# An early expert's units and its rest's run, reordered into one pipeline of turn, next up product, down product

## The chip, the cores and the metric

The kernel runs on 1 core of one Trainium2 chip. Its time is device microseconds (us) of one execution: 428.04 us is the median of three runs (427.71 to 428.32). Fewer is better.

## The reference

Three layers follow each other. The inputs are float32.

```python
# 1. attention in a sliding window: q, k, v (2, 8, 576, 64)
scores = q @ k.T / sqrt(64), kept where 0 <= i - j < 64; softmax; @ v
x = heads laid side by side -> (1152, 512)
# 2. mixture of experts: w_gate (512, 8), w1 (8, 512, 1024), w2 (8, 1024, 512)
logits = x @ w_gate; e = argmax(logits); gate = softmax(logits)[e]
row i goes to expert e[i], at most cap = 288 rows per expert, in order of i
out[i] = gate[i] * (relu(x[i] @ w1[e]) @ w2[e]), or 0 for a row past cap
# 3. dense layer: w_in (512, 2048), w_out (2048, 512)
h = x @ w_in; g = h * clip(h + 3, 0, 6) / 6; out = g @ w_out
```

## The kernel before, in words

**Attention and routing.** The rows go through the attention in nine blocks of 128. The operations are nodes of a planner written in the kernel (`node`, `run_nodes`): each has a priority, an estimated cost on TensorE (PE), ScalarE (A), VectorE (V), GpSimd (P) or the DMA queue (D), the nodes that it needs, and a ring of buffers that it takes and frees. The planner picks the node that can start first by its own clock and writes it into the engines' queues. Each engine then runs its queue in that order.

**The early expert.** After five of nine blocks (`NE = 5`) the expert with most rows so far is known. Its first 128 rows are gathered, scaled, turned (transposed by TensorE, `early_turn`) into `xTE`, and its weights, 8 half weights of 512 KB, are loaded into `wE` (tile `early`). An expert has four units (`NFU = 4`) of 256 hidden columns. A unit is an up product (`early_up`, two nodes `e0`, `e1`, of two chunks each), a relu to the tile `first_w` (`early_relu`, `er`), two transposes of the hidden rows (`early_hidden`, `et`), a copy (`early_hidden_out`, `eh`) and a down product (`early_down`, nodes `e2`, `e3`). These products are in full float32. The first `NEU = 2` units are nodes of the planner. The other two are written by hand after it: `own_up` (up product and relu) and `own_end` (transposes, copy, down product).

**The rest's run.** When all nine blocks are routed, experts are ranked (`ranks`, `slots`, `slot_index`), and the rows that the early expert's rank still has (`REST`) are gathered (`first_gather`, node `g0`, tile `first_w`). `rest_turn` scales them on VectorE and turns them into `xTR`. The run then uses the same eight half weights again: four units of `own_up` and `own_end` with `rest = True`. The order by hand is: up product of one unit, then `own_end` of the unit before it; `rest_turn` stands between the up product of the last early unit and the `own_end` of the one before. In three of the rest's units `own_end` also scales and turns a block of rows of the first team (`between`: `prep_scale`, `prep`). Behind each of the rest's units come three steps of `aside`, the index arithmetic of the compact order, on VectorE.

**The teams and the dense layer.** The other seven experts run in three teams (`TEAMS`), each a large expert ("w", `ws_stage`, two steps per unit) beside one or two small ones ("a", "b", `ts_stage` or `tiny_stage`), in the order of the strings `ORDER`. Their matrices are split: a float32 half weight in a buffer `raw` (8 of them, `NRAW`) is cast to a reduced format on ScalarE (line 252) and the remainder taken on VectorE (line 257), into `wt`, and a product is three passes. Last comes the dense layer (`d_stage`); its weights are first made out of 64-bit words by six operations on ScalarE and VectorE (`conv64`, lines 200 to 223), then split. Units 0 and 1 of the dense layer are loaded and made early, between the experts' units, at the places `FIRST_AT` and `SECOND_AT`; they are tiles `wt_fixed` and `first_w`.

**What orders the loads and splits.** From here on a second planner keeps an estimate of each engine's time (`est`, `spend`). Loads, conversions and splits are jobs with a due unit. `fill(limit)`, called wherever an engine will wait anyway, writes jobs into the queues as long as they start by the estimate before that limit; it does this only while `live[0]` is set. `need` forces a job out when a product wants it. A load counts as landed 3.5 us after its issue (`load_job`, `conv_job`).

Of the kernel before, what the change touches and what calls it, by code (L numbers as in the profile page):

```python
# [23 lines left out]
def tile_kernel(ctx, tc, q, k, v, w_gate, w1, w2, w_in, w_out, out, cap):  # L24
# [74 lines left out]
    def bank(tag):  # L99
        n = BANKS[tag][turn_at[tag] % len(BANKS[tag])]  # L100
        turn_at[tag] += 1
        return banks[:, n, :]
# [129 lines left out]
    NFU = F // FU  # L232
# [35 lines left out]
            nc.sync.dma_start(t.rearrange("p (k d) -> p k d", d=DM), src)  # L268


    NEU = 2
    x2f = xp2.tile([128, 2 * NC * XW], F32, name="early", tag="x2")
    wE = [x2f[:, HALF * i : HALF * i + HALF] for i in range(2 * NFU)]
    xTE, xTR = (
# [40 lines left out]
    with ExitStack() as actx:  # L315
# [25 lines left out]
        for i in range(2):  # L341
            r = slice(64 * i, 64 * i + 64)
# [53 lines left out]
        def node(name, prio, engs, fn, needs=(), take=None, free=(), lag=LAG):  # L396
            engs = {e: c * CS.get(name[0] if isinstance(name, tuple) else name, 1.0) for e, c in engs.items()}
            nodes[name] = (prio, engs, fn, needs, take, free, lag)
# [59 lines left out]
        box = {}  # L458
# [359 lines left out]
        def early_up(u, i):  # L818
            def run(e):
                if i == 0:  # L820
                    box["uE", u] = bank("s")[:, 0:FU]
                pairs = [(xTE[:, c, :], wE[2 * u][:, c * FU : c * FU + FU]) for c in (2 * i, 2 * i + 1)]
                mm(box["uE", u], pairs, start=(i == 0), stop=(i == 1))

            return run

        def early_part(u):
            return slice(FU * (u % 2), FU * (u % 2) + FU)
# [13 lines left out]
        def early_hidden(u):  # L842
            def run(e):
                box["vE", u] = pt = bank("s")[:, 0:FU]
                hf = box["hfE"][:, early_part(u)]
                for kf in range(2):
                    nc.tensor.transpose(pt[:, 128 * kf : 128 * kf + 128], hf[:, 128 * kf : 128 * kf + 128], ident)

            return run
# [42 lines left out]
                node(("wl", u, h), p + 2 * u + h, {"D": 1.3}, early_load(u, h), ["pl"], lag=2.0)  # L892
        for u in range(NEU):
            o = p + PRIO["ear"] + 2 * u
            node(("e0", u), o, {"PE": 0.86}, early_up(u, 0), ["xE", ("wl", u, 0)], "s")
            node(("e1", u), o, {"PE": 0.86}, early_up(u, 1), [("e0", u)])
            node(("er", u), o, {"A": 0.27, "V": 0.34}, early_relu(u), [("e1", u)], None, [("s", ("e0", u))])
            node(("et", u), o, {"PE": 0.22}, early_hidden(u), [("er", u)], "s")
            node(("eh", u), o, {"A": 0.27, "V": 0.34}, early_hidden_out(u), [("et", u)], None, [("s", ("et", u))])
            needs = [("eh", u), ("wl", u, 1)] + [("e3", u - 1)] * (u > 0)  # L900
            node(("e2", u), o + 1, {"PE": 0.86}, early_down(u, 0), needs, None if u else "x")
            node(("e3", u), o + 1, {"PE": 0.86}, early_down(u, 1), [("e2", u)])

# [108 lines left out]

    NWT = 4
    NRAW = 8
    FIRST_AT = (0, 4, 4, 4)
    SECOND_AT = (7, 7, 17, 19)
    NPC = 4
    EOFF = (mybir.EngineType.Activation, mybir.EngineType.DVE)
# [21 lines left out]
        steps.append((kind, s, f, unit_of[key], last))  # L1040


    ORDER = ('wwawwawawaww', 'awawwwwawaww', 'awbwwbwaaawbbwww')
    for n, (small, b) in enumerate(TEAMS):
        at_ = dict.fromkeys("abw", 0)
        order = ORDER[n]
# [24 lines left out]
    def spend(e, cost, ready=0.0):  # L1071
        est[e] = max(est[e], ready) + cost
        return est[e]
# [43 lines left out]
    def take_raw(m, h):  # L1117
        r_raw.take()
        raw_t[m, h] = rawp.tile([128, HALF], F32, name="raw")

    def load_job(m, h):
        _, s, u = units[m]

        def gate():
            return r_raw.free(raw_at[m, h])

        def run(e, fin):
            take_raw(m, h)
            if u == 0:
                e_of[s] = expert(s)  # L1130
            weights_in(raw_t[m, h], e_of[s], u, h)
            raw_ready[m, 2 * h] = raw_ready[m, 2 * h + 1] = fin + 3.5
            if whole(m):
                half_ready[m, h] = fin + 3.5
            return fin

        return [({"D": 1.46}, gate, run)]

    def conv_job(m, i):
        u = units[m][2]  # L1140
        ix = {}
        first = m == dense0 + 1
        b, (load, c_abs, c_round, *mid, t_add) = conv64(u, i, first_w[i] if first else None)

        def run_load(e, fin):
            r_raw.take()
            load()
            raw_t[m, i] = first_w[i] if first else b["lo"].bitcast(F32)
            return fin + 3.5

        def run_abs(e, fin):
            ix["ct"] = r_ct.take()
            c_abs()
            return fin

        def plain(fn):
            def run(e, fin):
                fn()
                return fin + 0.13

            return run

        def run_add(e, fin):
            t_add()
            r_ct.rel[ix["ct"]] = fin
            if first:
                r_raw.rel[raw_at[m, i]] = fin
            raw_ready[m, i] = fin + 0.2
            return fin + 0.2

        now = lambda: 0.0
        ops = [({"D": 1.46}, lambda: r_raw.free(raw_at[m, i]), run_load), ({"A": 0.6}, r_ct.free, run_abs)]
        ops.append(({"A": 0.57}, now, plain(c_round)))
        ops += [({"V": c}, now, plain(fn)) for c, fn in zip((0.34, 0.34, 0.61), mid)]
        ops.append(({"V": 0.61}, now, run_add))
        return ops
# [54 lines left out]
    def advance(fits):  # L1231

        for j in jobs:
            costs, gate, run = j[2][0]
            r = gate()
            if r is None:
                continue
            r = max(r, j[3])
            e = min(costs, key=lambda e: max(est[e], r) + costs[e] + BIAS.get(e, 0.0))
            t = max(est[e], r)  # L1240
            if not fits(j, e, t, costs[e]):
                continue
            j[3] = run(e, spend(e, costs[e], r))
            j[2].pop(0)
            if not j[2]:
                jobs.remove(j)
            return True
        return False
# [67 lines left out]
    def prep_scale(s, i, ready=0.0):  # L1316
        x_ready[s, i] = scale(xg[s, i], 3 * RANKS[s] + i, ready)
# [544 lines left out]
        ring.rel = [t] * ring.n  # L1862
    for _ in range(NFIRST):
        assert advance(lambda j, e, t, c: e == "D")

    spend("D", 0.8, done["g0"] - 2.3)
    for n, (s, i, _) in enumerate(rows_at[:3]):
# [17 lines left out]
    def own_up(rest, u):  # L1885

        key = "uR" if rest else "uE"
        t = xTR if rest else xTE
        box[key, u] = bank("rot")[:, 0:FU]
        mm(box[key, u], [(t[:, c, :], wE[2 * u][:, c * FU : c * FU + FU]) for c in range(NC)])  # L1890
        r = spend("PE", 1.83, box["rR"] if rest else done["wl", u, 0]) + 0.2
        fill(r)
        nc.scalar.activation(box["hfE"][:, early_part(u)], box[key, u], AF.Relu)
        return spend("A", 0.27, r) + 0.2

    def own_end(rest, u, r):
        pt = bank("rot")[:, 0:FU]
        hf, h = (box[n][:, early_part(u)] for n in ("hfE", "hE"))
        for kf in range(2):
            nc.tensor.transpose(pt[:, 128 * kf : 128 * kf + 128], hf[:, 128 * kf : 128 * kf + 128], ident)  # L1900
        r = spend("PE", 0.22, r) + 0.2
        fill(r)
        nc.scalar.copy(h, pt)
        r = spend("A", 0.27, r) + 0.2
        for fn in between.pop((rest, u), []):
            fn()
        if rest and u == 0:
            box["aR"] = bank("acc")
        acc = box["aR" if rest else "aE"]
        pairs = [(h[:, 128 * kf : 128 * kf + 128], wE[2 * u + 1][:, DM * kf : DM * kf + DM]) for kf in range(2)]  # L1910
        mm(acc, pairs, start=(rest and u == 0), stop=(u == NFU - 1))
        r = spend("PE", 1.75, max(r, done["wl", u, 1])) + 0.2
        fill(r)
        if u == NFU - 1:
            key = "yR" if rest else "yE"
            box[key] = y = first_w[2 if rest else 3]
            nc.scalar.copy(y, acc)
            box[key, "at"] = spend("A", 0.52, r) + 0.2

    between = {}  # L1920
    for n, (s, i, _) in enumerate(rows_at[:3]):
        between[True, n] = [
            lambda s=s, i=i, n=n: prep_scale(s, i, done["g0"] + 2.2 * (n + 1)), lambda s=s, i=i: prep(s, i, "t")
        ]
    before = None
    for rest, u in [(False, u) for u in range(NEU, NFU)] + [(True, u) for u in range(NFU)]:
        r = own_up(rest, u)
        if not rest and u == NFU - 1:
            rest_turn()
        if before:  # L1930
            own_end(*before)
        if rest:
            for _ in range(3):
                next(aside)
        before = rest, u, r
    own_end(*before)
    for step_, key, off_at in ((0, "yE", None), (1, "yR", lambda: off_of(REST))):
        at(step_, to_dense, box[key], off_at, box[key, "at"])
    x2 = xp2.tile([128, 2, NC, XW], F32R, name="x2", tag="x2")
# [67 lines left out]
```

## Time and profile before

| | before |
|---|---|
| median of three runs | 428.04 us |
| profiled execution | 429.9 us |
| its span, first to last instruction | 428.2 us |
| TensorE busy | 406.6 us, 95% |
| VectorE busy | 281.3 us, 66% |
| ScalarE busy | 234.1 us, 55% |
| GpSimd busy | 49.7 us, 12% |
| mean granted TensorE clock | 0.992 |

Rows below are from this one execution. PE is TensorE's matmul, PEld its weight load, DVE VectorE, ACT ScalarE, POOL GpSimd, SPq the queue of SyncE, which issues the loads. A row of a timeline has the start, the time to the end of the last instruction in it, the engine, the line of the kernel, the operation, what it writes and reads, and how many instructions were merged; in square brackets the idle time of the engine before it and who ended that. Matmuls are pipelined, so a row's time is a little longer than the distance to the next row; that distance is what a product takes. Line 238 is the helper of all matrix products, so the tiles tell them apart.

### The profile page before, as it was taken

To read this page: it belongs to the slowest core of one execution; us is meant where nothing else is said; L and a number is where in the kernel's file an instruction comes from. 1 tells how busy PE (TensorE), PEld (TensorE's weight loads), DVE (VectorE), ACT (ScalarE), POOL (GpSimd) and SP (SyncE) were. 2 spreads that over 40 slices of the span, in tenths; PEclk is the share of its full clock that TensorE was granted. 3 is DMA by queue.
4 is the path that set the end of the run, shared out by engine and by line. 5 is a ranking of instruction groups with operands and counts; after the bars stand their busy time and mean duration, and the time that the engine had idled before them with its cause. 6 is when DMAs were issued, how large, how long until landed. Compare 5 with 4: busy or idle time off the path is not lost.

```text
span 428.2 us, 8357 instructions
## 1 busy us (share of the span) xinstructions
PE 406.6 (95%) x3031; PEld 343.7 (80%) x3031; DVE 281.3 (66%) x781; ACT 234.1 (55%) x510; POOL 49.7 (12%) x108
## 2 busy tenths in 40 slices
PE   7999788898999999999999999999999999999992
PEld 4877565455899899899889898888888888898981
DVE  2888967479779857977579999548896222322440
ACT  4877773466576737657687666348583222423330
POOL 8633404011001101000000000000000000120101
PEclk9999999899999999999999999999999999999998
DMA  9998766973568996989940090023410000110101
GB/s 172 210 219 193 265 231 212 372 218 114 197 200 273 282 337 201 341 267 325 312 150 2 21 364 10 0 94 104 149 51 0 2 0 0 51 49 2 49 27 55
DMA packets 63857, 65.49 MB, mean 153 GB/s; under 512 B 30688, under 2 KB 47072, under 8 KB 63808
## 3 DMA queue, kind: packets, MB, share of 16 engines
q1 hardware_dynamic: 62224, 59.79, 45.6%
q0 software_dynamic: 1584, 5.08, 3.3%
q8 instruction: 26, 0.43, 0.4%
q14 instruction: 23, 0.19, 0.1%
HBM read 60.15 MB, written 4.72 MB: 151 GB/s over the span
## 4 chain that ended last, share of the span: by engine, by line
PE 84%; DVE 8%; ACT 4%; issue 1%; DMA 1%; SPq 0%; POOL 0%; ACTq 0%; POOLq 0%; DVEq 0%
PE banks L238 71%; PE banks L1459 2%; PE banks L498 2%; PE banks L1484 2%; PE banks L616 2%; ACT pe L588 1%; PE banks L562 1%; DMA v_sb<-in_v_dram 1%; PE banks L598 1%; DVE neg L575 1%; PE banks L1295 1%; PE banks L528 1%; ACT wt L252 0%; DVE raw L223 0%; DVE c L216 0%
## 5 line engine op out<-in xcount | busy, mean ns | idle before, releaser
L238 PE MATMUL banks<-x,wt 128*128 128x320 f32 (+3 forms) x432 | 79.8, 336 | 0.0
L238 PEld LDWEIGHTS banks<-x,wt 128*128 128x128 f32 x432 | 70.8, 188 | 7.1
L257 DVE TENSOR_TENSOR wt<-raw,wt 128x512 fp32r<-128x512 f32 x100 | 64.6, 686 | 17.6 <-ACT wt L252 15.3
L238 PE MATMUL banks<-wt,g 128*128 128x512 f32 x288 | 69.6, 390 | 0.0
L1548 DVE SCALAR_TENSOR_TENSOR gf<-r,banks 128x320 f32<-128x320 f32 (+3 forms) x48 | 26.6, 554 | 60.6 <-ACT r L1545 60.5
L1545 ACT ACTIVATE r<-banks,c_three 128x320 f32<-128x320 f32 (+3 forms) x48 | 28.0, 583 | 69.7 <-PE banks L238 69.6
L238 PEld LDWEIGHTS banks<-wt,g 128*128 128x128 f32 x288 | 53.7, 188 | 10.6
L252 ACT CAST wt<-raw 128x512 fp32r<-128x512 f32 x100 | 58.8, 629 | 5.4 <-PE banks L238 3.2
L238 PE MATMUL banks<-xT,wt 128*128 128x256 f32 (+2 forms) x288 | 38.4, 283 | 0.0
L238 PE MATMUL banks<-h,wt 128*128 128x256 f32 (+2 forms) x288 | 37.1, 279 | 0.0
L238 PEld LDWEIGHTS banks<-xT,wt 128*128 128x128 f32 x288 | 35.0, 192 | 1.9 <-DVE h L1355 0.8
L238 PEld LDWEIGHTS banks<-h,wt 128*128 128x128 f32 x288 | 34.6, 192 | 0.3 <-issue 0.3
L1554 DVE TENSOR_TENSOR g<-gf,g 128x320 fp32r<-128x320 f32 (+2 forms) x40 | 23.4, 584 | 10.4 <-ACT g L1551 9.6
L1551 ACT CAST g<-gf 128x320 fp32r<-128x320 f32 (+2 forms) x40 | 21.3, 533 | 14.6 <-DVE gf L1548 14.5
L1591 POOL DMA_INDIRECT out_dram<-raw,cidx x4 | 4.2, 1040 | 206.4 <-DVE raw L1585 197.9
L238 PE MATMUL banks<-x,wt_fixed 128*128 128x320 f32 (+3 forms) x144 | 26.8, 337 | 0.1
L200 ACT ACTIVATE c<-raw 128x512 f32<-128x512 f32 x32 | 21.6, 675 | 7.4 <-DVE raw L223 5.9
L238 PEld LDWEIGHTS banks<-x,wt_fixed 128*128 128x128 f32 x144 | 23.5, 188 | 2.7 <-ACT x L1375 0.5
L238 PE MATMUL banks<-wt_fixed,g 128*128 128x512 f32 x96 | 23.2, 390 | 0.0
L588 ACT ACTIVATE pe<-neg,nmx 128x128 f32<-128x128 f32 x72 | 22.3, 392 | 0.1
L216 DVE SCALAR_TENSOR_TENSOR c<-raw,c 128x512 uint32<-128x512 uint32 x32 | 22.0, 688 | 0.5
L575 DVE CUSTOM_DVE_ANT_0 neg<-banks,tmask 128x128 f32<-128x128 f32 x72 | 16.2, 285 | 9.1 <-PE banks L562 9.1
(298 smaller groups left out, 636.8 us busy)
## 6 DMA issues: line engine op xcount, KB each, us to landing
raw<-in_moe_w_dram SPq DMA_DIRECT2D x56, 512.0 KB, 6.5
raw<-in_moe_w_in_dram SPq DMA_DIRECT2D x16, 512.0 KB, 5.1
raw<-in_moe_w_out_dram SPq DMA_DIRECT2D x16, 512.0 KB, 5.9
early<-in_moe_w_dram SPq DMA_DIRECT2D x8, 512.0 KB, 5.3
x_dram<-xt SPq DMA_DIRECT2D x9, 256.0 KB, 2.8
q_sb<-in_q_dram SPq DMA_DIRECT2D x8, 256.0 KB, 4.1
k_sb<-in_k_dram SPq DMA_DIRECT2D x8, 256.0 KB, 4.8
v_sb<-in_v_dram SPq DMA_DIRECT2D x8, 256.0 KB, 5.1
```

The lines of the kernel that those rows point to most:

```text
L200: nc.scalar.activation(box["c"].bitcast(F32), box["hi"].bitcast(F32), AF.Abs)
L216: nc.vector.scalar_tensor_tensor(out=box["c"], in0=box["hi"], scalar=0xC0000000, in1=box["c"], op0=ALU.bitwise_and, op1=ALU.bitwise_or,)
L238: nc.tensor.matmul(out, l, r, start=(start and n == 0), stop=(stop and n == len(pairs) - 1))
L252: nc.scalar.copy(hi, r)
L257: V.tensor_tensor(out=lo, in0=r, in1=hi.bitcast(F32), op=ALU.subtract)
L498: nc.tensor.transpose(pt[:, hp, :], t[:, 2 * hp : 2 * hp + 2, :].rearrange("p h d -> p (h d)"), ident)
L575: V.tensor_tensor_reduce(out=neg[:, hp, :], in0=box["sp", g][:, hp, :], in1=tmask[:, first, :], scale=-1.0, scalar=3.0e38, op0=ALU.add, op ...
L588: nc.scalar.activation(pe[:, hp, :], neg[:, hp, :], AF.Exp, bias=nmx[:, hp : hp + 1], scale=-1.0)
L1545: nc.scalar.activation(r, ph, AF.Relu, bias=c_three)
L1548: V.scalar_tensor_tensor(out=gf, in0=r, scalar=6.0, in1=ph, op0=ALU.min, op1=ALU.mult)
L1551: nc.scalar.copy(hi, gf)
L1554: V.tensor_tensor(out=lo, in0=gf, in1=hi.bitcast(F32), op=ALU.subtract)
```

## The change

It does five things. (1) `NEU` goes from 2 to 3, and the needs of the planner's nodes change: the up product of unit 2 comes after the hidden transposes of unit 1, the transposes of unit 0 after the up product of unit 1, and the down product of unit 1 after the up product of unit 2. The transposes and down product of unit 2 are left to the part by hand. (2) That part, for units 2 and 3 and the rest's four, now writes for each: the hidden transposes and copy (`own_hidden`), the up product of the next unit (`own_up`), then its own down product (`own_down`). The rest's rows are turned behind the up product of early unit 3. A block of the team's rows is scaled in one unit of the rest and turned in the next, ahead of the down product. (3) `live[0]` is off from the first two loads until the rest's rows are turned, so no split and no further job is written before. (4) In the plan a load counts as landed 6.5 us after its issue while three to twelve have been taken, 3.5 us otherwise. (5) `FIRST_AT` and two strings of `ORDER` have other values.

```diff
-    NEU = 2
+    NEU = 3
...
         for u in range(NEU):
             o = p + PRIO["ear"] + 2 * u
-            node(("e0", u), o, {"PE": 0.86}, early_up(u, 0), ["xE", ("wl", u, 0)], "s")
+            needs = ["xE", ("wl", u, 0)] + [("et", u - 1)] * (u > 1)
+            node(("e0", u), o, {"PE": 0.86}, early_up(u, 0), needs, "s")
...
-            node(("et", u), o, {"PE": 0.22}, early_hidden(u), [("er", u)], "s")
+        for u in range(NEU - 1):
+            o = p + PRIO["ear"] + 2 * u
+            node(("et", u), o, {"PE": 0.22}, early_hidden(u), [("er", u)] + [("e1", 1)] * (u == 0), "s")
...
-            needs = [("eh", u), ("wl", u, 1)] + [("e3", u - 1)] * (u > 0)
+            needs = [("eh", u), ("wl", u, 1)] + [("e3", u - 1), ("e1", u + 1)] * (u > 0)
...
-    FIRST_AT = (0, 4, 4, 4)
+    FIRST_AT = (1, 2, 3, 5)
...
-    ORDER = ('wwawwawawaww', 'awawwwwawaww', 'awbwwbwaaawbbwww')
+    ORDER = ('wwawwawwaaww', 'aawwwwwawaww', 'awbwwbwaaawbbwww')
...
+    def landing(fin):
+
+        return fin + (6.5 if 2 < len(raw_t) <= 12 else 3.5)
...
-            raw_ready[m, 2 * h] = raw_ready[m, 2 * h + 1] = fin + 3.5
+            raw_ready[m, 2 * h] = raw_ready[m, 2 * h + 1] = landing(fin)
...
     for _ in range(NFIRST):
         assert advance(lambda j, e, t, c: e == "D")
+    live[0] = False
...
-    def own_end(rest, u, r):
+    def own_hidden(rest, u, r):
...
-        r = spend("A", 0.27, r) + 0.2
-        for fn in between.pop((rest, u), []):
-            fn()
+        return spend("A", 0.27, r) + 0.2
+
+    def own_down(rest, u, r):
         if rest and u == 0:
             box["aR"] = bank("acc")
+        h = box["hE"][:, early_part(u)]
...
-    before = None
-    for rest, u in [(False, u) for u in range(NEU, NFU)] + [(True, u) for u in range(NFU)]:
-        r = own_up(rest, u)
-        if not rest and u == NFU - 1:
+    own = [(False, u) for u in range(NEU - 1, NFU)] + [(True, u) for u in range(NFU)]
+    r_up = done["er", NEU - 1]
+    for n, (rest, u) in enumerate(own):
+        r = own_hidden(rest, u, r_up)
+        if rest and u < 3:
+            s, i, _ = rows_at[u]
+            prep_scale(s, i, done["g0"] + 2.2 * (u + 1))
+        if n + 1 < len(own):
+            r_up = own_up(*own[n + 1])
+        if rest and u:
+            prep(*rows_at[u - 1][:2], "t")
+        if not rest and u == NFU - 2:
             rest_turn()
-        if before:
-            own_end(*before)
+            live[0] = True
+        own_down(rest, u, r)
         if rest:
             for _ in range(3):
                 next(aside)
-        before = rest, u, r
-    own_end(*before)
```

## Rows read from the trace of the kernel before

**Rows 1.** Busy us (instructions) by stretch: PE, PEld, DVE, ACT, POOL; granted clock, DMA share, GB/s

```profile
61.73:77.40 15.67, 13.14 (x84) 8.93 (x82) 10.98 (x50) 6.19 (x19) 4.35 (x5) 1.00 0.61 205
77.40:104.72 27.32, 23.50 (x84) 14.13 (x85) 18.53 (x54) 15.94 (x34) 3.91 (x3) 0.94 0.75 241
77.34:110.10 32.76, 28.03 (x116) 17.98 (x116) 23.71 (x65) 19.39 (x41) 3.91 (x3) 0.95 0.64 205
...
110.16:140.00 29.84, 29.84 (x230) 28.60 (x231) 24.02 (x54) 19.32 (x42) 1.92 (x2) 1.00 0.75 245
140.00:221.50 81.50, 81.40 (x734) 72.85 (x732) 59.95 (x128) 53.16 (x121) 2.53 (x2) 1.00 0.89 288
```

**Rows 2.** Chain of waits in order of time: start us, us, what

```profile
109.50 0.61 DVE x L1403
...
221.49 199.00 PE banks L238 x1008
```

**Rows 3.** Timeline of TensorE, 61.6 to 112 us

```profile
70.17 0.44 PE L847 MATMUL banks<-ident,first_w 128*128 128x128 f32 x2 [0.47 <-ACT first_w L836]
71.32 0.39 PE L972 MATMUL banks<-A1t,A 128*128 128x48 f16 x9 [0.71 <-DVE A1t L967]
...
73.34 3.62 PE L238 MATMUL banks<-early 128*128 128x256 f32 x16
77.40 0.66 PE L1879 MATMUL banks<-ident,first_w 128*128 128x128 f32 x4 [0.44 <-DVE first_w L1287]
78.73 0.44 PE L1900 MATMUL banks<-ident,first_w 128*128 128x128 f32 x2 [0.68 <-ACT early L1882]
79.63 3.23 PE L238 MATMUL banks<-early,first_w 128*128 128x512 f32 x4 [0.46 <-ACT first_w L1903]
82.65 2.39 PE L238 MATMUL banks<-early 128*128 128x256 f32 x8
...
85.84 1.98 PE L238 MATMUL banks<-early,first_w 128*128 128x512 f32 x4 [0.58 <-ACT first_w L1903]
...
95.16 0.66 PE L1295 MATMUL banks<-ident,xg 128*128 128x128 f32 x4 [0.58 <-ACT first_w L1903]
95.65 1.88 PE L238 MATMUL banks<-early,first_w 128*128 128x512 f32 x4
97.37 1.89 PE L238 MATMUL banks<-early 128*128 128x256 f32 x8
99.09 0.38 PE L1900 MATMUL banks<-ident,first_w 128*128 128x128 f32 x2
...
104.72 2.00 PE L238 MATMUL banks<-xT,wt 128*128 128x256 f32 x12
```

**Rows 4.** The same busy table as rows 1, by single microseconds

```profile
78.00:79.00 1.00, 0.32 (x3) 0.20 (x2) 0.00 (x0) 0.59 (x1) 0.00 (x0) 1.00 1.02 380
...
81.00:82.00 1.00, 1.00 (x3) 0.48 (x2) 0.97 (x3) 0.22 (x1) 0.00 (x0) 0.50 1.06 379
...
84.00:85.00 1.00, 1.00 (x7) 0.83 (x5) 0.00 (x0) 0.00 (x0) 0.00 (x0) 1.00 1.04 372
```

**Rows 5.** Timeline of VectorE, 72 to 77.4 us

```profile
72.26 1.29 DVE L257 TENSOR_TENSOR wt<-raw,wt 128x512 fp32r<-128x512 f32 x2
...
76.25 0.69 DVE L257 TENSOR_TENSOR wt<-raw,wt 128x512 fp32r<-128x512 f32 x1 [0.84 <-ACT wt L252]
76.86 0.48 DVE L1287 TENSOR_SCALAR first_w<-first_w,sgate 128x512 f32<-128x512 f32 x1
```

**Rows 6.** Timeline of GpSimd: the gather of the rest's rows

```profile
69.24 0.94 POOL L793 DMA_INDIRECT first_w<-x_dram,sidx  x1 [16.27 <-DVE sidx L991]
```

**Rows 7.** Tile of the teams' gathered rows, 60 to 125 us: their gathers' landing

```profile
DMA to landing us min/median/max: 3.4/6.1/8.1
```

**Rows 8.** Tile of the half weights, 60 to 112 us: their loads' landing

```profile
DMA to landing us min/median/max: 5.9/7.5/9.1
```

**Rows 9.** Timeline of ScalarE: one cast of a split

```profile
74.07 0.62 ACT L252 CAST wt<-raw 128x512 fp32r<-128x512 f32 x1 [1.97 <-issue]
```

More of the change, by code (lines that the diff above doesn't have):

```diff
@@ L1131, in run @@
             weights_in(raw_t[m, h], e_of[s], u, h)
-            raw_ready[m, 2 * h] = raw_ready[m, 2 * h + 1] = fin + 3.5
+            raw_ready[m, 2 * h] = raw_ready[m, 2 * h + 1] = landing(fin)
             if whole(m):
-                half_ready[m, h] = fin + 3.5
+                half_ready[m, h] = landing(fin)
             return fin
@@ L1148, in run_load @@
             raw_t[m, i] = first_w[i] if first else b["lo"].bitcast(F32)
-            return fin + 3.5
+            return landing(fin)
         def run_abs(e, fin):
@@ L1918, in own_end @@
             box[key, "at"] = spend("A", 0.52, r) + 0.2
[L1920 to L1924, printed above, removed]
-    before = None
-    for rest, u in [(False, u) for u in range(NEU, NFU)] + [(True, u) for u in range(NFU)]:
-        r = own_up(rest, u)
-        if not rest and u == NFU - 1:
+    own = [(False, u) for u in range(NEU - 1, NFU)] + [(True, u) for u in range(NFU)]
[10 more added lines that the diff above has]
+        if not rest and u == NFU - 2:
             rest_turn()
-        if before:
-            own_end(*before)
+            live[0] = True
+        own_down(rest, u, r)
         if rest:
```

## The prediction

> **What bounds the kernel now.** I read the page's busy shares first: TensorE is busy 95% of the span, so time can only come from stretches where it stands still or runs slow. The chain of waits, in order of time, says where. Its last long piece, 221.49 to 420.5, is the dense layer on TensorE alone; before it, up to 110.1, the chain runs on VectorE [rows 2]. Then the busy table by stretch: 29.84 of 29.84 us from 110.16 to 140, 81.40 of 81.50 up to the dense layer, but 23.50 of 27.32 between 77.40 and 104.72, at a mean granted clock of 0.94, and 13.14 of 15.67 in the stretch before [rows 1]. So the early expert and the rest's run are the only place with something to win, and 3.8 + 2.5 us of idle time and what the clock takes are the most that is there.
>
> TensorE's own timeline shows each loss. Unit by unit it issues the transposes of the hidden rows just after ScalarE has the relu to do, and the down product just after the copy: waits of 0.47 (70.17), 0.68 (78.73), 0.46 (79.63), 0.58 (85.84) and 0.58 (95.16) on ScalarE, and 0.71 on VectorE at 71.32 [rows 3]. At 77.40 it waits for the rest's rows: VectorE scales them at 76.86, directly behind a weight split of 0.69 that started at 76.25, and that split waited 0.84 for ScalarE [rows 5]. After this thin stretch (busy 0.32 between 78 and 79) the granted clock falls to 0.50, the lower of the two levels (1.2 GHz), and is back at 1.00 by 84 [rows 4].
>
> **The change, part by part.** The sum is made against the profiled execution (429.9 us, span 428.2), and its difference is taken off the median of 428.04; the 1.9 us between the two are not touched.
>
> *Up to the rest's turn.* The work ahead of it stays four up and two down products, plus the transposes of unit 2, which come forward (0.44 by the pair at 70.17). The new order, up 0, up 1, both pairs of transposes, up 2 and down 0, down 1, gives ScalarE a product's time for each relu and copy, so 0.47 of the waits goes here; the routing's 0.71 goes too, if a product stands before it [rows 3]. TensorE is done with up 3 at 76.96 in the profile (73.34 + 3.62), then at 76.96 + 0.44 - 0.47 - 0.71 = 76.2; I count another 0.5 for the second such wait that the same order removes, an estimate from the 0.47: 75.7. The other side is the gather of the rest's rows, issued at 69.24 [rows 6]; gathers landed 3.4 to 8.1 us after issue, median 6.1 [rows 7]. That is 75.3, and with the scale and the hand-over of 0.54 (76.86 to 77.40) 75.9. With no split on VectorE ahead of it nothing else holds it. I take the turn at 76.0: a gain of 1.4, between -0.5 (landing after 8.1 us: 77.9) and 1.7 (75.7).
> The Trainium skill, "DMA: Bandwidth & Descriptors", section "Queues, rings and completion order", has each DMA engine take turns between queue rows packet by packet. By it the rows' gather shares with the weight loads and does not queue behind them, so the dense weights' load that no longer stands beside it would bring the landing forward only by its share; no row here shows the gather of the rest landing, so the sum leaves that at nothing.
>
> *From the turn to the first team's step.* In the profile 77.40 to 104.72, 27.32 us. The work: six down and four up products at 1.72 (95.65 to 97.37 is a down product, 97.37 to 99.09 an up one), four turns of rows at 0.49 (95.16 to 95.65), five pairs of transposes at half of that, 0.25, and 0.1 that the last down product still waits for its copy (the wait of 0.58 less the turn that now stands beside it) [rows 3]. 17.2 + 2.0 + 1.2 + 0.1 = 20.5. So 6.8 goes: ScalarE's copies, relus and the copy of the turned rows (0.59) now run beside a product of 1.72. In that 6.8 stands the clock: the down product took 3.23 instead of 1.98 and the up product 2.39 instead of 1.89 [rows 3], 1.75 together.
>
> *The splits that move.* Four weight splits ran before the turn (two from 72.26, one at 76.25 and one between) in time that VectorE had free [rows 5]; they come after it now, 4 x 0.69 = 2.8 us of VectorE, and the same number of casts on ScalarE. From 77.34 to 110.10 VectorE is busy 23.71 of 32.76 [rows 1]; it then has 26.5 us of work in a shorter stretch. Their price lies between 0 (VectorE's 9.05 us of idle time take them) and 8.2 (they and what queues behind them cost all that was gained). Queued behind a split on VectorE are the scaling of the next rows and the low halves that the first team's products read; behind a cast on ScalarE, the next relu and copy. I take the moved work in full, 2.8, since the chain shows VectorE as the last to be ready at 110.1 already now.
>
> *Edits at nothing.* Later landings in the plan, dense pieces loaded a unit later, and the order of two teams' steps move work in 110 to 221, where TensorE is busy without a break and VectorE 24.02 of 29.84 [rows 1]: TensorE's own queue hides them. If that cover is gone, each costs the wait of a half weight behind its load, which the rivals price. The gathers on GpSimd and the loads on SyncE stay in their order; the first load after the eight buffers waits for the first split, later than now.
>
> The sum: 1.4 + 6.8 - 2.8 = 5.4 us. 429.9 - 5.4 = 424.5 for the profiled execution, 428.04 - 5.4 = **422.6 us** for the median.
>
> **Rivals.**
> *Cover holds (419.8).* VectorE's idle time takes all moved splits: the whole 8.2 is won. For it: 9.05 us idle. Against: the plan fills each gap anyway, and the index arithmetic of the compact order is on VectorE without a place in the plan.
> *The clock falls anyway (424.4).* TensorE stands still for a moment before the turn in the new order too. The clock fell after a stretch of many gaps, none over 0.7 us [rows 3, 4]. If it falls, 1.75 comes back: 422.6 + 1.75. The Trainium skill, "TensorE: Matmul & The Clock Gate", section "Why this matters for your kernels", asks only that long idle gaps between bursts be avoided; by that rule a short wait here would cost nothing, but the profile's fall without one long gap speaks against reading it so.
> *VectorE becomes the bound (426.4).* 26.5 us of work from 76.0 on, of 9.05 us idle two thirds (6.0) stay because VectorE still waits for casts and landings: ready at 108.5 instead of 110.1, a gain of 1.6.
> *Casts that wait for loads (430.0, slower).* ScalarE takes its work in order, and a cast whose weight has not landed stands ahead of a relu or copy of the pipeline. The profile has such a wait of 1.97 at 74.07 [rows 9]. The plan now counts 6.5 us from issue for most of these loads; they took 5.9 to 9.1, median 7.5 [rows 8]. Six half weights are split in the pipeline's time. At 1.7 us each that reaches TensorE, 10.2 is lost against 8.2 won: 2.0 slower. It decides from 8.2 / 6 = 1.4 us each. Against it: most loads will have waited long before their cast, since no cast comes before the turn.
>
> **How the numbers follow.** This kernel's runs spread by 0.14% (427.71 to 428.32), and 0.2% (0.86 us) is what can be told from no change. Chances: forecast 0.46, cover holds 0.16, clock falls 0.12, VectorE bound 0.14 (0.10 of it beyond 0.2%, 0.04 within), loads 0.12. Faster 0.46 + 0.16 + 0.12 + 0.10 = 0.84, same 0.04, slower 0.12. The range reaches from just under "cover holds" to beyond the VectorE case and leaves the slower one out: 419.0 to 427.8.
>
> **What would show it.** The turn of the rest's rows near 76.0 and no split before it; down products of 1.98 throughout and a granted clock of 1.00 between 76 and 98; no waits on ScalarE in front of the transposes and down products; the first team's step near 97 to 100 instead of 104.72; the dense layer starting near 216 instead of 221.49. I am wrong if the pipeline's products stand behind casts or VectorE's scaling, or if the team steps show gaps that they do not have now.

## The result, and the profile after

| | before | after |
|---|---|---|
| median, 4 runs of each on one chip | 428.0 us (427.71 to 428.32) | 424.55 us (422.93 to 424.68) |
| ratio, with its 95% interval | | 0.9911 [0.9886, 0.9936] |
| profiled execution, its span | 429.9, 428.2 us | 424.58, 422.9 us |
| TensorE, VectorE, ScalarE, GpSimd busy | 406.6, 281.3, 234.1, 49.7 us | 404.4, 280.5, 234.1, 49.1 us |

The change is 3.5 us faster in the median; forecast were 5.4. In the two profiled executions it is 5.3 us of span, as forecast, but that agreement is luck: it is made of two misses that cancel, shown below.

TensorE's timeline of the changed kernel, from the rest's turn to the first team's steps (the same columns as [rows 3]; lines of the kernel have moved by 3 to 8):

```profile
75.61 0.60 PE L1887 MATMUL banks<-ident,first_w 128*128 128x128 f32 x4
76.04 1.88 PE L238 MATMUL banks<-early,first_w 128*128 128x512 f32 x4
...
94.14 1.98 PE L238 MATMUL banks<-early,first_w 128*128 128x512 f32 x4
95.56 1.99 PE L238 MATMUL banks<-xT,wt 128*128 128x256 f32 x12
...
102.27 0.66 PE L1399 MATMUL banks<-ident,first_w 128*128 128x128 f32 x4 [2.85 <-DVE h L1362]
102.87 2.08 PE L238 MATMUL banks<-wt,xT 128*128 128x256 f32 x12
104.75 2.75 PE L238 MATMUL banks<-h,wt 128*128 128x256 f32 x12
107.31 1.62 PE L238 MATMUL banks<-xT,wt 128*128 128x256 f32 x12
```

The turn stands at 75.61 with no wait in brackets, the down products take 1.88 to 1.98, and the first team's step starts at 95.56, where [rows 3] have 104.72. Then TensorE waits 2.85 us, at the turn of the rest's finished rows into the dense layer's input (102.27), for VectorE's low half `h` (line 1362: the remainder of the first team's hidden tile, after its relu in the reduced format). The turn reads none of `h`. It writes a bank of the ring `rot`, which has three (`"rot": (0, 1, 2)` in the kernel), and by the order of the kernel's calls that is the bank in which the first team's product stood; the low half is the last to read it. So this is a wait for a buffer, and a longer ring was not tried. Behind the wait a product of 1.6 takes 2.75. The busy table by stretch (columns of rows 1) says the same in sums:

```profile
61.31:75.61 14.30, 12.87 (x88) 9.26 (x85) 8.61 (x46) 3.92 (x15) 4.00 (x5) 1.00 0.53 167
75.61:95.56 19.95, 19.92 (x83) 13.02 (x82) 14.63 (x35) 16.07 (x34) 3.35 (x3) 1.00 0.85 297
95.56:102.87 7.31, 4.46 (x35) 3.84 (x33) 6.81 (x26) 2.94 (x7) 0.31 (x1) 1.00 0.60 203
102.87:110.21 7.34, 7.34 (x50) 7.34 (x49) 5.12 (x12) 3.38 (x7) 0.00 (x0) 0.77 0.48 150
```

The second line is the pipeline: 19.92 of 19.95 us busy, for work that took 27.32 [rows 1] (less one pair of transposes, some 0.25, that now stands ahead of the turn). The third and fourth lines are what is given back. The same two stretches of the kernel before:

```profile
104.72:110.16 5.44, 4.53 (x35) 3.85 (x33) 5.24 (x11) 3.38 (x7) 0.00 (x0) 1.00 0.06 21
110.16:116.00 5.84, 5.84 (x48) 5.84 (x49) 3.41 (x10) 2.38 (x5) 0.00 (x0) 1.00 0.95 327
```

So the balance is: 0.42 that was there already at 61.31 (61.73 before; executions of the kernels below differ by as much at this point, so it is not a gain of the change), 1.37 up to the turn (15.67 less 14.30), 7.37 in the pipeline (27.32 less 19.95), together 9.16; then 7.31 instead of 5.44, 1.87 lost, and 7.34 instead of 5.84 at a granted clock of 0.77, 1.50 lost. That leaves 5.8 us at 110.21 (116.00 before), and of it the dense layer starts 5.5 us earlier, at 216.00 instead of 221.49 [rows 2]: the stretch between is alike but for 0.3. The chain of waits of the changed kernel has the low half of the wait and the start of the dense layer:

```profile
101.88 0.34 DVE h L1362
...
216.00 194.94 PE banks L238 x990
```

What makes the low half late stands on two engines. ScalarE's timeline of the changed kernel:

```profile
100.51 0.65 ACT L252 CAST wt_fixed<-raw 128x512 fp32r<-128x512 f32 x1 [3.77 <-DVE raw L223]
101.07 0.38 ACT L1359 ACTIVATE h<-banks 128x256 fp32r<-128x256 f32 x1
```

VectorE's:

```profile
73.01 0.70 DVE L1294 TENSOR_SCALAR first_w<-first_w,sgate 128x512 f32<-128x512 f32 x1 [1.43 <-DMA first_w<-x_dram,sidx]
...
77.38 2.53 DVE L257 TENSOR_TENSOR wt<-raw,wt 128x512 fp32r<-128x512 f32 x4 [3.66 <-ACT wt L252]
...
99.74 0.69 DVE L223 CUSTOM_DVE_ANT_0 raw<-raw,c 128x1024 uint16<-128x1024 uint16 x1
...
101.19 0.69 DVE L257 TENSOR_TENSOR wt_fixed<-raw,wt_fixed 128x512 fp32r<-128x512 f32 x1 [0.43 <-ACT wt_fixed L252]
101.80 0.42 DVE L1362 SCALAR_TENSOR_TENSOR h<-banks,h 128x256 fp32r<-128x256 f32 x1
```

A cast of a dense piece (`wt_fixed`) is next in ScalarE's queue and waits 3.77 us for the end of that piece's conversion on VectorE (line 223). The relu behind it, which the low half needs, comes at 101.07; with no cast ahead of it, it runs at 97.42 (*cast on VectorE*, below). And the low half itself stands behind that piece's conversion and split in VectorE's queue, and behind the index arithmetic, whose last step ahead of it ends at 99.8. This is a piece of the dense layer, whose product is 115 us away. SyncE's queue shows why it is here. The loads of the dense layer's first four pieces (two of `w_in`, two of `w_out`; start, time to the end of the last issue, the queue, line, operation and tile) in the kernel before:

```profile
68.73 0.47 SPq L191 DMA_DIRECT2D raw<-in_moe_w_in_dram  x1
88.98 0.38 SPq L191 DMA_DIRECT2D raw<-in_moe_w_in_dram  x1
90.58 0.94 SPq L194 DMA_DIRECT2D raw<-in_moe_w_out_dram  x2
```

and of the changed kernel:

```profile
73.44 0.46 SPq L191 DMA_DIRECT2D raw<-in_moe_w_in_dram  x1
75.29 0.47 SPq L191 DMA_DIRECT2D raw<-in_moe_w_in_dram  x1
84.36 0.35 SPq L194 DMA_DIRECT2D raw<-in_moe_w_out_dram  x1
101.91 0.35 SPq L194 DMA_DIRECT2D raw<-in_moe_w_out_dram  x1
```

The first piece comes 5 us later, the second 14 us and the third 6 us earlier, the fourth 11 us later. That is `FIRST_AT`: its four numbers are the team units behind which the pieces' loads are queued, and (0, 4, 4, 4) to (1, 2, 3, 5) moves two of them later (the first and the fourth) and two of them forward.

The kernel before has such pieces ahead of its own first low half too. Its VectorE and TensorE:

```profile
107.29 1.28 DVE L257 TENSOR_TENSOR wt_fixed<-raw,wt_fixed 128x512 fp32r<-128x512 f32 x2
108.49 0.41 DVE L1355 SCALAR_TENSOR_TENSOR h<-banks,h 128x256 fp32r<-128x256 f32 x1
108.96 0.66 PE L1392 MATMUL banks<-ident,first_w 128*128 128x128 f32 x4 [0.37 <-DVE h L1355]
```

There the slower pipeline left VectorE more time: the first team's step starts at 104.72 and waits only 0.37 at this turn and 0.54 behind it. The faster pipeline reaches the step 9 us earlier, and with the pieces moved forward as well VectorE is not done with them.

### The profile page after: what moved, and what is told of

It reads as the page before. It is cut to its first block, busy times and chain, and to the rows that moved or that the text cites. A ratio compares the mean times of both kernels' runs of the same rounds, so it can differ in the third digit from the quotient of the medians.

```text
span 422.9 us, 8358 instructions
## 1 busy us (share of the span) xinstructions
PE 404.4 (96%) x3031; PEld 344.5 (81%) x3031; DVE 280.5 (66%) x781; ACT 234.1 (55%) x510; POOL 49.1 (12%) x108
## 4 chain that ended last, share of the span: by engine, by line
PE 83%; DVE 7%; DMA 4%; ACT 2%; issue 1%; SPq 1%; POOL 0%; ACTq 0%; POOLq 0%; DVEq 0%
PE banks L238 70%; PE banks L1466 2%; PE banks L1491 2%; PE banks L498 2%; DMA c<-x_dram,eI 2%; PE banks L616 2%; DMA v_sb<-in_v_dram 1%; PE banks L598 1%; PE banks L562 1%; SPq L466 1%; DMA out_dram<-part,cidx 1%; DVE neg L575 1%; PE banks L1302 1%; PE banks L528 1%; DVE xT L1308 0%
## 5 line engine op out<-in xcount | busy, mean ns | idle before, releaser
L238 PE MATMUL banks<-h,wt 128*128 128x256 f32 (+2 forms) x288 | 38.3, 285 | 0.0
L238 PEld LDWEIGHTS banks<-h,wt 128*128 128x128 f32 x288 | 35.8, 198 | 0.5 <-issue 0.5
```

What stands on the lines that cost most here:

```text
L238: nc.tensor.matmul(out, l, r, start=(start and n == 0), stop=(stop and n == len(pairs) - 1))
```

## The experiments

Twelve kernels were timed in five rounds each, beside the kernel before on the same chip: four in a first comparison (before 427.9 us), four in a second (427.78), four in a third (429.4). In the third, 6 of the 11 runs of before have the mean granted clock of 0.992 that goes with the fall of [rows 4], against 2 of 11 in the first and 1 of 9 in the second, so in the third the ratio flatters a little, and times within that group are the better comparison. Below, the hold is part (3) of the change (`live[0]` off until the rest's rows are turned), the places are the four numbers `FIRST_AT`, the turn by itself is that of the rest's rows into `xTR`, and the wait is the one in front of the later turn of the finished rows into dense rows, 2.85 in the changed kernel.

**No hold.** Splits may be written before the turn again, all else as changed:

```diff
-    live[0] = False
```

> The changed kernel with one part undone: splits may be written before the rest's rows are turned. Theory A (VectorE is the last to be ready at the end of the pipeline, and the four splits that the hold moved behind the turn are part of its queue): VectorE has 3.66 us free before its first split in the changed kernel; up to 2.8 us of splits go there, the turn comes at most 0.9 us later than 75.61, and the wait of 2.85 us at 99.4 shrinks by 1 to 2.8; 422 to 424 us against the changed kernel's 424.55. Rival B (the hold is what makes the pipeline run: splits and casts in front of the scaling and the copies): the turn comes at 76.5 to 77.4, waits on ScalarE come back, 425.5 to 427.

425.15 us (423.93 to 425.86), ratio 0.9923 [0.9903, 0.9943]. TensorE's timeline:

```profile
76.85 0.66 PE L1886 MATMUL banks<-ident,first_w 128*128 128x128 f32 x4 [1.03 <-DVE first_w L1294]
...
102.47 0.66 PE L1399 MATMUL banks<-ident,first_w 128*128 128x128 f32 x4 [1.69 <-DVE h L1362]
103.66 2.93 PE L238 MATMUL banks<-wt,xT 128*128 128x256 f32 x12 [0.54 <-DVE x L1410]
```

The turn waits 1.03 for the scale behind the splits, and the later wait shrinks from 2.85 to 1.69 + 0.54. The clock falls here too: the product behind the wait takes 2.93. The two waits cancel, and the interval overlaps that of the changed kernel: with the new load places the hold is worth nothing that can be told.

**Order only.** The pipeline alone: no hold, `FIRST_AT`, `ORDER` and the landing of before.

```diff
-    FIRST_AT = (1, 2, 3, 5)
+    FIRST_AT = (0, 4, 4, 4)
...
-    ORDER = ('wwawwawwaaww', 'aawwwwwawaww', 'awbwwbwaaawbbwww')
+    ORDER = ('wwawwawawaww', 'awawwwwawaww', 'awbwwbwaaawbbwww')
...
-        return fin + (6.5 if 2 < len(raw_t) <= 12 else 3.5)
+        return fin + 3.5
...
-    live[0] = False
```

> The new order of the units alone: no hold, and the load places, step order and landing times of the kernel before. Theory A (the order makes the gain; the other four parts are worth less than 1 us together): first team step within 1 us of 95.56, 423.5 to 425.5. Rival B (the order without the hold and the new load places stands behind casts and landings): first team step at 98 or later, 426 to 428.

422.04 us (421.77 to 422.44), 0.9857 [0.9836, 0.9878]: 2.5 us under the whole change, and under the range of both theories. The turn still waits 1.03 behind splits, later waits are 0.59 and 0.54, and in the profiled execution the clock holds. So the order of the units by itself gains 5.9 us, and some of the other edits cost time.

**Order and hold.** The same with the hold kept (the diff above without its last line).

> The new order with the hold, and the load places, step order and landing times of the kernel before: it differs from the order alone (422.04) by the hold only. Theory A (the hold moves four splits, 2.8 us of VectorE, behind the turn; VectorE is the last to be ready): turn near 75.6 instead of 76.67, but the first low half of a hidden tile later than 100.71 by 1 to 2 us, a wait of 1.5 to 3 us and the clock falls: 423.5 to 425. Rival B (the other three parts cost the 2.5 us, the hold is free or wins the 1.0 us of the turn): 421 to 422.2.

420.34 us (419.76 to 420.71), 0.9825 [0.9812, 0.9839]. TensorE's timeline:

```profile
75.99 0.66 PE L1887 MATMUL banks<-ident,first_w 128*128 128x128 f32 x4 [0.27 <-DVE first_w L1294]
...
99.75 0.60 PE L1399 MATMUL banks<-ident,first_w 128*128 128x128 f32 x4
100.44 1.70 PE L238 MATMUL banks<-wt,xT 128*128 128x256 f32 x12
```

No wait is left behind the turn. The hold, which I had charged with 2.8, wins 1.7 (422.04 to 420.34; the runs lie apart, the intervals of the ratios, from two comparisons, just touch). My theory for this run fell and the rival's mechanism was right; the time came out 0.7 under the rival's range. Why the held splits cost nothing is on VectorE's timeline of *order only*. There the four splits run before the turn, and VectorE stands idle behind it:

```profile
80.32 0.43 DVE L207 TENSOR_SCALAR c<-c 128x512 f32<-128x512 f32 x1 [3.71 <-ACT c L200]
```

With the hold the idle time stands in front of the turn (3.91, for the rows' gather), and the splits fill what was idle behind it.

**Places as before.** One line of the changed kernel goes back:

```diff
-    FIRST_AT = (1, 2, 3, 5)
+    FIRST_AT = (0, 4, 4, 4)
```

> The changed kernel with the old places of the dense unit's four loads (0, 4, 4, 4 instead of 1, 2, 3, 5). Theory A (the new places bring a second dense piece's conversion and split, 2.9 us of VectorE, ahead of the first team's hidden tiles): one split wt_fixed less ahead of the first low half, wait at the rest's second turn below 1.5 us, 421.5 to 423.5. Rival B (the hold is the cause): 424 to 425.

420.96 us (420.47 to 421.83), 0.9838 [0.9825, 0.9852]. The places alone cost 3.6 in the median; against the one run of the changed kernel without a fall of the clock (422.93) it is 2.0, so some 1.6 of it is the clock. VectorE's timeline:

```profile
75.81 0.49 DVE L1294 TENSOR_SCALAR first_w<-first_w,sgate 128x512 f32<-128x512 f32 x1 [4.27 <-DMA first_w<-x_dram,sidx]
...
99.42 0.42 DVE L1362 SCALAR_TENSOR_TENSOR h<-banks,h 128x256 fp32r<-128x256 f32 x1
```

The second piece, loaded at 92.21, is converted only after 102; the low half is at 99.42 instead of 101.80, and TensorE turns the rest's finished rows at 100.12 without a wait. But the gather lands later, since a third load goes out before it again. The DMA view of this kernel (tiles, queue, operation, count, median us from issue to landing):

```profile
first_w<-x_dram,sidx POOLq DMA_INDIRECT x1, 7.1
```

and of the changed kernel:

```profile
first_w<-x_dram,sidx POOLq DMA_INDIRECT x1, 4.2
```

The scale starts at 75.81 instead of 73.01 and the rest's first turn waits 0.64. The new places buy that 0.64, and lose the 2.85 later and, in most runs, the clock.

**Places between.** Only the two pieces that had moved forward go back:

```diff
-    FIRST_AT = (1, 2, 3, 5)
+    FIRST_AT = (1, 4, 4, 5)
```

> The changed kernel with the dense unit's loads at 1, 4, 4, 5: the first piece stays where the change has it, the second and third go back. Theory A (the second piece's conversion ahead of the first team step is what costs): one split wt_fixed ahead of the first low half, no wait above 0.6 us at the rest's second turn, 420.3 to 421.5, as with the old places (420.96). Rival B (the first piece's place matters): 422.5 or more.

420.99 us (420.42 to 421.3), 0.9813 [0.979, 0.9836], against 424.63 for the changed kernel in the same comparison. TensorE's wait at the turn into dense rows:

```profile
100.01 0.66 PE L1399 MATMUL banks<-ident,first_w 128*128 128x128 f32 x4 [0.71 <-DVE h L1362]
```

So it is the second and third piece, queued earlier (the two were not tried one by one), that cost the 3.6. The first piece's later load keeps its gain (scale at 73.16); what it wins at the turn, the wait of 0.71 takes, a little more than theory A allowed (0.6).

**Landing as before.** The plan counts 3.5 us for every load:

```diff
-        return fin + (6.5 if 2 < len(raw_t) <= 12 else 3.5)
+        return fin + 3.5
```

> The changed kernel with every load counted as landed 3.5 us after its issue. Theory A (landing times only shift what is written when; the backlog of VectorE is the same): 424 to 425. Rival B (casts then stand before their load has landed and hold up ScalarE's relus and copies): waits on ScalarE in the pipeline, 425.5 or more. Rival C (the later landings push splits into the crowded end): 421.5 to 423.5.

422.81 us (422.65 to 424.12), 0.9884 [0.9869, 0.9899]. The wait is 2.31. By the mean clocks the clock fell in one of the four compared runs, in the changed kernel in three of four; most of the 1.7 between the medians is that (the three runs without it take 422.65 to 422.97, the changed kernel's one 422.93). The intervals overlap, and this run does not show that the estimate of the landing matters.

**Index early.** The index arithmetic of the compact order, twelve steps on VectorE that the plan has no place for, is written right behind the turn, where VectorE stands idle for 3.66 us from 73.7 in the changed kernel:

```diff
             rest_turn()
+            for _ in range(12):
+                next(aside)
             live[0] = True
         own_down(rest, u, r)
-        if rest:
-            for _ in range(3):
-                next(aside)
```

> The changed kernel with the twelve steps of index arithmetic all written right behind the scaling of the rest's rows, where VectorE is idle for 3.66 us, and none between the rest's units. Theory A (the lost gain is VectorE's queue: some 4 us of arithmetic that the plan does not count): the wait of 2.85 us at 99.4 goes, and with it the fall of the clock behind it (about 1.6 us); 420 to 421. Rival B (ScalarE's casts and the landings of weights set the end of that chain): the wait stays above 1.5 us, 423.5 to 424.6.

419.70 us (419.53 to 420.08), 0.9803 [0.9785, 0.9821], the lowest median here, 8.2 us under before and 0.3 under the range of theory A. TensorE's timeline:

```profile
75.50 0.60 PE L1887 MATMUL banks<-ident,first_w 128*128 128x128 f32 x4
...
99.16 0.60 PE L1399 MATMUL banks<-ident,first_w 128*128 128x128 f32 x4
```

VectorE's:

```profile
73.81 0.22 DVE L1720 TENSOR_TENSOR tns<-rse,cntS 128x64 f32<-128x64 f32 x1
...
78.29 0.16 DVE L1766 TENSOR_TENSOR top_f<-offF,ks 128x8 f32<-128x8 f32 x1
78.42 0.69 DVE L257 TENSOR_TENSOR wt<-raw,wt 128x512 fp32r<-128x512 f32 x1
...
97.70 0.69 DVE L257 TENSOR_TENSOR wt_fixed<-raw,wt_fixed 128x512 fp32r<-128x512 f32 x1 [0.46 <-ACT wt_fixed L252]
98.31 0.42 DVE L1362 SCALAR_TENSOR_TENSOR h<-banks,h 128x256 fp32r<-128x256 f32 x1
```

The dense pieces come as early as in the changed kernel (75.04 for the second), with the same split ahead of the low half, and now no wait is left: the work of 73.8 to 78.4 is out of the way and the low half is 3.5 us earlier (98.31 for 101.80). With the old places, order and landing beside it (**index, old places**) it stays so:

> The early index arithmetic (419.7 with the changed kernel's places) with the old load places, step order and landing times, hold on. If VectorE's queue is the whole story, both have it empty enough and TensorE is without a gap from the turn on: 419.3 to 420.2, the same. If the new places help once the queue is short, 420.5 to 422.

419.94 us (419.65 to 420.17), 0.982 [0.9806, 0.9833]. The two intervals overlap: once VectorE's idle stretch is used, places, order and landing together make no difference that can be told.

**Before, with the index early.** The same move in the kernel before, without the pipeline:

```diff
             rest_turn()
+            for _ in range(12):
+                next(aside)
...
-        if rest:
-            for _ in range(3):
-                next(aside)
```

> The kernel before, with the twelve steps of index arithmetic right behind the scaling of the rest's rows. Theory A (before the change TensorE waits on ScalarE at every unit; VectorE's queue is second): waits of the pipeline stay, those on VectorE (0.72, 0.37, 0.54) go, 426 to 427.6. Rival B (VectorE's queue was the bound already, so the order of the units is not what won): 424.5 or less.

426.14 us (425.92 to 426.83), 0.994 [0.9916, 0.9963]. ScalarE's waits of [rows 3] stay, two of them here:

```profile
78.14 0.44 PE L1900 MATMUL banks<-ident,first_w 128*128 128x128 f32 x2 [0.68 <-ACT early L1882]
79.03 1.98 PE L238 MATMUL banks<-early,first_w 128*128 128x512 f32 x4 [0.46 <-ACT first_w L1903]
```

Against the five runs of before in this comparison without the low mean clock (427.63 to 428.16) the index move is worth some 1.9 us by itself, and the pipeline is what takes the ScalarE waits away. The waits at the turn are those of the kernel before, and still the down product takes 1.98 here and not 3.23: in this execution the clock does not fall.

**Cast on VectorE.** The casts of dense pieces go from ScalarE to VectorE, so that no relu stands behind one:

```diff
-        return [({"A": 0.56}, gate, run_high), ({"V": 0.62}, lambda: 0.0, run_low)]
+        return [({"V": 0.62} if m == dense0 else {"A": 0.56}, gate, run_high), ({"V": 0.62}, lambda: 0.0, run_low)]
```

> The changed kernel with the casts of the first dense unit's four pieces on VectorE instead of ScalarE. In the changed kernel ScalarE stands 3.77 us at such a cast, which waits for VectorE's conversion, and the first team step's relu behind it starts at 101.07 although its product ended near 97.5. Theory A (ScalarE, held up by that cast, makes the wait): the relu starts near 98, the wait of 2.85 falls below 1.5, 422 to 423.6. Theory B (the length of VectorE's queue makes it, whoever casts): with 0.6 us more on VectorE per cast the first low half comes at 101.8 or later, 424.5 to 426.

423.44 us (423.09 to 423.75), 0.9874 [0.9851, 0.9898]. The relu is free at 97.42 instead of 101.07, but the low half comes at 100.79 and TensorE still waits 2.00. The clock falls behind this wait in the profiled execution. The result is mixed: with ScalarE's blocked cast gone the wait is 0.85 shorter, and the 2.00 that stay are VectorE's own queue, which runs without a gap from 88.5 up to the low half. It is no clean division, since the run also puts a cast of 0.42 on VectorE and the second piece's split behind the low half.

**Warm wait.** Twelve products of constants, whose result nobody reads, fill the wait, so that TensorE does not stand still:

```diff
     def to_dense(y, off, ready, t0=0, t1=128):
 
+        if y is box.get("yR"):
+            for _ in range(12):
+                nc.tensor.matmul(banks[:, 5, :], c_ones, c_low.rearrange("p a b -> p (a b)")[:, 0:512], start=True, stop=True)
```

> The changed kernel with twelve 128x512 products of constants, used by nobody, on TensorE ahead of the rest's turn into the dense rows, where it stands still for 2.85 us. Theory A (the fall of the clock at 104 to 107 us follows from that wait): granted clock 1.00 throughout, about 1.6 us less, 422.9 in every run. Rival B (the fall has another cause, or the added work lasts longer than the wait): 424.5 or more.

423.23 us (422.96 to 423.40), 0.9882 [0.9864, 0.99]. TensorE's timeline:

```profile
99.76 2.54 PE L1397 MATMUL banks<-c_low,c_ones 128*128 128x512 bf16 x11
102.55 0.66 PE L1402 MATMUL banks<-ident,first_w 128*128 128x128 f32 x4 [0.25 <-DVE h L1362]
...
104.69 1.60 PE L238 MATMUL banks<-h,wt 128*128 128x256 f32 x12
```

The turn into dense rows is no earlier (102.55), but the product behind it takes 1.60 instead of 2.75, and the mean clocks of all five runs (0.994 to 0.996) give no sign of the fall. In the median that is 424.55 - 423.23 = 1.3 us; the changed kernel's own runs lie 1.6 apart, three at 424.5 to 424.7 and one at 422.93. The intervals of the two ratios overlap, so what this run shows is the clock more than the time.

**The change once more.**

> The changed kernel once more, beside the others. If the fall of the clock behind the wait of 2.85 us comes and goes, its runs lie in two groups, near 424.6 at a mean clock of 0.990 to 0.992 and near 422.9 at 0.996 or more; median 422.9 to 424.6.

424.63 us (423.15 to 426.0), 0.9906 [0.9878, 0.9935]. Two of the runs are at 423.15 and 423.26 with a mean granted clock of 0.996 to 0.997, the others at 424.26 to 426.0 with 0.986 to 0.990. The expectation had the second group at 424.6 alone; two runs at 0.986 lie 1.0 to 1.4 above it, and no trace shows what those lost. Its profiled execution is one without the fall:

```profile
102.43 0.66 PE L1399 MATMUL banks<-ident,first_w 128*128 128x128 f32 x4 [2.87 <-DVE h L1362]
...
104.56 1.60 PE L238 MATMUL banks<-h,wt 128*128 128x256 f32 x12
```

The same wait, the same code, and the clock stays at 1.00.

## Why the prediction was right in direction and too large in size

**Right: the pipeline.** The waits on ScalarE are gone, the down products take 1.88 to 1.98, and the stretch from the turn takes 19.95 where I counted 20.5 (27.32 before). Up to the first team's step 9.2 us are won, 0.42 of them there at the start of the stretch: 8.7 against 8.2 for this part of the sum. The reorder alone gives it (*order only*: step at 96.73), and the index move alone does not (*before, with the index early*: step at 101.89).

**Right: the turn, in its time.** 76.0 was forecast, 75.61 measured (76.0 without the 0.42 of the start). But I had the gather as what sets it, and TensorE's own work does. The gather landed early because one load fewer goes out before it: 4.2 to 4.8 us after its issue in the five executions that give a landing with two loads ahead of it (4.2 in the changed kernel, 4.5 in *places between*), against 6.5 to 7.1 in the four with three (7.1 in *places as before*, 6.7 in *order and hold*). I had left this at nothing. The Trainium skill, "DMA: Bandwidth & Descriptors", section "Queues, rings and completion order", says that queue rows share an engine in turns; the trace agrees as far as a load beside the gather slows it, and the size, 1.7 to 2.9 us of landing, stands in these runs alone.

**Failed: "Edits at nothing".** I wrote that the dense pieces are loaded a unit later and act in 110 to 221, under TensorE's own queue. The trace of the kernel before already contradicts the second half: its dense pieces are converted and split from 81 on, three of the splits between 107.29 and 109.5, ahead of 110. And only the first and last piece are loaded later. The second and third move forward by two units and one, the second's load by 14 us, and its conversion and split, and a part of the third's conversion, fall ahead of the first team's low half at 101.80. Cost: 3.6 us (424.55 to 420.96, and 424.63 to 420.99), some 1.6 of it the fall of the clock behind the new wait. It was there to be read in the four numbers of the diff and in the kernel's table of load places.

**Failed: "The splits that move", 2.8.** The moved splits don't cost; holding them back wins 1.7 with the old places (*order only* to *order and hold*) and makes no difference that can be told with the new ones. The rival "cover holds", 419.8, is about where the kernel comes out when the places (420.96; 420.34 with `ORDER` and the landing) or the index arithmetic (419.70, 419.94) are out of the way: VectorE's idle time does take the moved work. The bound is not the amount of VectorE's work but where it stands: in the changed kernel VectorE is idle 3.66 us from 73.7, and then has the index arithmetic and a far unit's piece ahead of the one instruction whose end frees the bank that TensorE wants.

**Mis-sized: the clock.** I took 1.75 of clock in the 6.8 from the profiled execution of before and carried it to the median. The four runs of before in the result give no sign of it: they take 427.71 to 428.32 us, as the runs at a mean clock of 0.994 and more do in the three comparisons (427.25 to 428.3), while those at 0.992 take 429.2 to 430.4. So the median could not win it. *Before, with the index early* has the same waits at the turn and no fall. Instead the changed kernel, in most runs, has a fall of its own at 104 to 107, behind the new wait:

```profile
104.00:105.00 1.00, 1.00 (x7) 1.00 (x7) 0.37 (x2) 0.08 (x2) 0.00 (x0) 0.50 0.70 283
```

Compared without falls on either side, before is at 427.25 to 428.3 and changed at 422.93 to 423.26, some 4.8 apart. The profile's 5.3 met the forecast of 5.4 by luck, in sum only: 9.2 won instead of 8.2, the 1.75 of clock among it, and 3.9 given back instead of 2.8, for other reasons (1.87 at the wait, 1.50 of clock, 0.5 in what follows).

**Of the rivals**, "the clock falls anyway" had the right number (424.4) by luck: the fall came not at the turn but 29 us later, behind a wait that the rival did not have. "VectorE becomes the bound" had the right engine and 1.9 us too much of it. "Casts that wait for loads" did not come: the casts that held up a relu waited for VectorE's conversion, not for a landing.

**Open.** *Order and hold* and *places as before* differ in `ORDER` and the landing together and their intervals overlap; `ORDER` alone was not tried, nor a ring of more than three banks. Whether the fall comes in a given execution, nothing in these traces tells.

## What to carry to other kernels

A reorder that speeds one engine moves the next wait: before counting the gain, list what each in-order queue holds ahead of the first instruction that the bottleneck will want next, and move work that is due far later, or work that the plan does not count, into a stretch where that engine stands idle. The first instruction wanted may be the last reader of a buffer, and not a producer of data. A table of load places is read number by number, since a load that moves forward brings its conversion and its casts with it. And a clock fall in one profiled execution is looked for in the mean clocks of the timed runs before it enters a sum against the median.

## What the runs showed of the hardware

The fall of the granted clock to 0.50 (1.2 GHz) is not a property of the code alone. By the mean clocks and the times, the kernel before has it in its profiled execution and in 2 of 11, 1 of 9 and 6 of 11 runs of the three comparisons, but in none of the 4 runs that the result rests on; the changed kernel has it in 3 of 4 and 4 of 6 runs, with a wait of 2.85 us in front in the profiled execution where it falls and 2.87 in the one where it does not. Of the other profiled executions with the new pipeline it fell behind waits of 2.31 (*landing as before*), 2.00 (*cast on VectorE*) and 1.69 + 0.54 (*no hold*), and not in the five where every wait behind the first team's step was at most 0.71, nor in *order only* (0.59 and 0.54). Where TensorE was kept busy through the wait, it fell in none of five runs. And the landing of one small gather (128 rows of 2 KB) moved from 4.2 us to 7.1 with a single further load of 512 KB issued just before it; over nine executions it is 4.2 to 4.8 against 6.5 to 7.1.
